# Banded attention and a softplus MLP on one core: quarter products in six token tiles, V rounded by its transfer, a maximum kept by the mask

## The chip, the cores and the metric

The kernel runs on one core of one Trainium2 chip. The core's engines each work through their own queue: TensorE (PE, matrix products, results in PSUM), VectorE (DVE), ScalarE (ACT), GpSimd (POOL) and SyncE (SP, which here only issues transfers). The metric is the device time of one execution in microseconds. Before the change it is 322.49 us, the median of 3 runs (322.43 to 322.93).

## The reference

The reference does attention with a band and a few global positions, reorders its result to tokens by features, and puts it through two matrix products with a softplus between them:

```python
def _attn_ref(q, k, v, global_idx):
    B, H, S, D = q.shape                       # 8, 8, 576, 64
    scores = (1.0 / np.sqrt(D)) * np.matmul(q, k.transpose(0, 1, 3, 2))
    mask = np.abs(pos[:, None] - pos[None, :]) <= 32
    mask = mask | is_global[:, None] | is_global[None, :]      # 8 global positions
    scores = np.where(mask, scores, -1000000000.0)
    scores = scores - np.max(scores, axis=-1, keepdims=True)
    attn = np.exp(scores)
    attn = attn / (np.sum(attn, axis=-1, keepdims=True) + 1e-09)
    return np.matmul(attn, v)

def _moe_ref(x, w_in, w_out):                  # x: 4608 x 512
    h = x @ w_in                               # 512 x 2048
    g = np.maximum(h, 0.0) + np.log1p(np.exp(-np.abs(h)))      # softplus
    return g @ w_out                           # 2048 x 512
```

## The kernel before

**Tiles.** The 4608 tokens are cut into 9 tiles of 512 (`m`, 0 to 8). The queries are cut into blocks of 32; a "pair" `n` (0 to 35, four per tile) is four such blocks with all 8 heads, and each block sees four key slots of 32 (previous, own, next, and the global keys). A batch `b` (0 to 7) is four and a half pairs.

**A pair's chain.** PE makes the scores (`s`, L1131) in two PSUM banks, one per half of the heads. For the first four pairs the mask is added by PE, DVE takes the maximum from PSUM, and ACT takes the exps with the maximum as a bias and keeps the sums (L1167). For the other 32 pairs DVE adds the mask on the way from PSUM to `st` (L1135, twice per pair) and takes the maximum (`m`, L1148), POOL subtracts it (L1154), ACT takes the exp of the whole pair (L1171), DVE sums it (`sm`, L1178) and inverts the sum (`rs`, L1180). Then POOL, for some pairs DVE, normalises into `pn` (L1186), DVE transposes it into `pt` (L1195), and PE multiplies with V (`xo`, L1297), which gives the token tile's input `xT` (L779). Rows of the global positions run beside it (`sg`, `pg`, `ov`, `vg`).

**A tile's products.** First product: for each of 16 column blocks of `w_in`, PE streams 512 tokens over 4 row blocks into `h` (L1334), and ACT writes the softplus to `g` (L1338), which exists once: the next tile's softplus overwrites it block by block. Second product, plain form (tiles 0 to 5): for each group of 128 tokens, 16 matmuls of 128x512 into one bank `o` (L1343), a copy to `osb` (L779) and a store. Second product in quarter products (tiles 6 to 8, `FAST = 6`, function `add_fast`): tokens, features and the inner dimension are halved, and the 2x2 by 2x2 block product is made from seven products of blocks instead of eight. Each of the seven is 8 x 2 matmuls of 128x256 (L1454). It needs four sums of quarters of `w_out`, made once, in two parts each (`add_sums`, "T"), and per tile four sums of quarters of `g`, in two parts each ("S", `combine`, L1403), made partly in place in `g` by DVE or POOL, each of them from the one before. Three of the results are added to an output on DVE (L1487). Sums of `w_out` lie in the staging buffers `stage` of q and k, and `s1` in that of V, so they wait until the last batch is loaded.

**Loads.** For batches 2 to 7, q, k and V come as fp32 into `stage` by SP's queue and are rounded to bf16 by POOL or ACT (`qk`, `vb`). V of batches 0 and 1 is rounded on its way by transfers that POOL issues (`load_rounded`, L500). `vb` exists twice. Stores of tiles 0 to 4 are issued by POOL, later ones by SP.

**What sets the order.** Each piece of work is recorded with `o.add` (its possible engines with costs, what it depends on, which buffers it opens and uses). `_Order.run` takes the pieces in the order that the table `ORDER` lists, each entry a piece and its engine, and emits them; each engine works in the order emitted. Up to 34 us of its own reckoning (`WARM`) it puts matmuls on an empty operand (`warm`, L786) into longer pauses of PE. The table is of the kernel itself; it is replaced whole.

Of the kernel before, what the change touches and what calls it, by code (L numbers as in the profile page):

```python
# [1658 lines left out]
```

## Time and profile before

| what | us |
|---|---|
| median of 3 runs | 322.49 (322.43 to 322.93) |
| the profiled execution's own time | 322.02 |
| its span, first to last instruction | 320.3 |
| PE busy | 309.9 (97%) |
| DVE busy | 249.0 (78%) |
| ACT busy | 229.7 (72%) |
| POOL busy | 217.7 (68%) |

The span is what the trace covers; the rest of an execution's time lies around it. In rows of a group (line, engine, operation, out<-in, shape, count) the numbers are busy us, mean ns of one, and the engine's idle time before them with what ended most of it. Rows of the chain of waits in order of time give start, us, and what ran, with its count. A matmul's own duration contains the pipeline's length: the streaming rate is read from a run of them in the chain.

### The profile page before, as it was taken

Reading aid. Unit: us, or ns where it says so; the run is one execution under the profiler, and the core shown is the slowest. Engines: PE = TensorE matmul, PEld = TensorE weight load, DVE = VectorE, ACT = ScalarE, POOL = GpSimd, SP = SyncE. Lnnn points to the kernel's source line nnn. Section 1 sums busy time; section 2 is a strip of 40 time slices with the busy share of each in tenths; the row PEclk is TensorE's granted clock in tenths of the full one; section 3 lists DMA queues with packets and bytes.
Section 4 is the critical chain, followed back from the end, with each engine's and each line's share of the span. In section 5 each row is a group of like instructions: output and inputs, shape, how many; then the busy total and the mean of one; then the engine's idle time right before and its main releaser. Section 6 shows DMA issues by size and latency. Waiting matters only on the chain.

```text
span 320.3 us, 12076 instructions
## 1 busy us (share of the span) xinstructions
PE 309.9 (97%) x5229; PEld 186.1 (58%) x5229; DVE 249.0 (78%) x438; ACT 229.7 (72%) x464; POOL 217.7 (68%) x186
## 2 busy tenths in 40 slices
PE   7889999999999999999999999999999999999995
PEld 6647965665565645544454455445544875685484
DVE  7987689976989898778988885897689666883063
ACT  7798847798698789579648946796199659726610
POOL 7994759892998687398788478499986385370220
PEclk9999999999999999999999999999999999999999
DMA  7999999999999899979996983710130010104003
GB/s 206 169 172 238 219 191 139 155 164 187 224 165 186 155 235 161 172 126 171 224 253 114 167 129 69 148 36 2 68 133 2 2 35 34 70 0 135 0 0 133
DMA packets 170335, 41.55 MB, mean 130 GB/s; under 512 B 153130, under 2 KB 168490, under 8 KB 170282
## 3 DMA queue, kind: packets, MB, share of 16 engines
q1 hardware_dynamic: 154920, 30.16, 49.5%
q0 software_dynamic: 15360, 10.62, 19.8%
q8 instruction: 41, 0.67, 0.9%
q14 instruction: 12, 0.10, 0.1%
q10 hardware_dynamic: 2, 0.00, 0.0%
HBM read 36.70 MB, written 9.44 MB: 144 GB/s over the span
## 4 chain that ended last, share of the span: by engine, by line
PE 89%; ACT 3%; POOL 3%; DMA 2%; DVE 1%; issue 0%; DVEq 0%; POOLq 0%
PE h L1334 38%; PE o L1343 27%; PE o L1454 11%; PE xo L1297 4%; PE s L1131 3%; DMA vb<-in_v_dram 2%; PE ov L1055 2%; POOL win L1525 2%; PE pick L945 1%; PE warm L786 1%; ACT st L1167 1%; ACT L1338 1%; PE sg L1029 1%; PE tr L913 1%; POOL pn L1186 1%; ACT g L1338 1%
## 5 line engine op out<-in xcount | busy, mean ns | idle before, releaser
L1334 PE MATMUL h<-xT,win 128*128 128x512 bf16 (+3 forms) x832 | 136.4, 313 | 1.4 <-ACT xT L779 0.7
L1338 ACT ACTIVATE g<-h 128x512 bf16<-128x512 f32 (+3 forms) x208 | 85.6, 490 | 35.1 <-PE h L1334 31.5
L1334 PEld LDWEIGHTS <-win 128*128 128x128 bf16 x832 | 70.7, 98 | 56.8 <-issue 3.1
L1343 PE MATMUL o<-wout,g 128*128 128x512 bf16 x384 | 93.3, 380 | 0.0
L1186 POOL TENSOR_TENSOR pn<-st,rs 128x1024 bf16<-128x1024 f32 (+1 forms) x40 | 68.7, 1736 | 31.2 <-DVE rs L1180 29.9
L1154 POOL TENSOR_TENSOR st<-st,m 128x1024 f32<-128x1024 f32 x32 | 60.4, 1895 | 24.9 <-DVE m L1148 23.9
L1343 PEld LDWEIGHTS <-g 128*128 128x128 bf16 x384 | 35.7, 98 | 39.5 <-issue 1.4
L1135 DVE TENSOR_TENSOR st<-s,mask 128x512 f32<-128x512 f32 x64 | 41.2, 678 | 12.2 <-PE s L1131 12.2
L1178 DVE TENSOR_REDUCE sm<-st 128x8 f32<-128x1024 f32 x32 | 38.3, 1196 | 2.2 <-ACT st L1171 2.0
L1148 DVE TENSOR_REDUCE m<-st 128x8 f32<-128x1024 f32 x32 | 38.3, 1206 | 0.3
L1171 ACT ACTIVATE st<-st 128x1024 f32<-128x1024 f32 x32 | 32.8, 1053 | 1.9 <-POOL st L1154 1.8
L1195 DVE STREAM_TRANSPOSE pt<-pn 128x512 int32<-128x512 int32 x36 | 24.6, 695 | 9.3 <-POOL pn L1186 9.2
L1454 PEld LDWEIGHTS <-g 128*128 128x128 bf16 x288 | 27.5, 98 | 5.7 <-ACT g L1338 0.3
L779 ACT COPY osb<-o 128x512 f32<-128x512 f32 x22 | 13.2, 600 | 13.6 <-PE o L1454 11.7
L779 ACT CAST xT<-xo 128x512 bf16<-128x512 f32 (+3 forms) x25 | 10.5, 475 | 15.2 <-PE xo L1297 15.1
L1338 ACT ACT_TABLE_LOAD x14 | 18.0, 1283 | 2.7 <-PE h L1334 2.4
L1454 PE MATMUL o<-wout,g 128*128 128x256 bf16 x144 | 19.5, 273 | 0.0
L1454 PE MATMUL o<-stage,g 128*128 128x256 bf16 x144 | 18.4, 273 | 0.0
L772 ACT ACTIVATE qk<-stage 128x1152 bf16<-128x1152 f32 (+1 forms) x14 | 16.9, 1217 | 1.6 <-DMA stage<-in_q_dram 1.6
L779 DVE CAST xT<-xo 128x512 bf16<-128x512 f32 (+3 forms) x27 | 12.6, 506 | 5.5 <-PE xo L1297 5.2
L1403 DVE TENSOR_TENSOR g<-g 128x1024 bf16<-128x1024 bf16 x8 | 7.8, 978 | 10.0 <-POOL stage L1403 9.9
L1171 ACT ACT_TABLE_LOAD x12 | 15.4, 1283 | 0.2
(145 smaller groups left out, 389.8 us busy)
## 6 DMA issues: line engine op xcount, KB each, us to landing
stage<-in_q_dram SPq DMA_DIRECT2D x48, 144.0 KB, 3.6
stage<-in_k_dram SPq DMA_DIRECT2D x48, 144.0 KB, 4.2
stage<-in_v_dram SPq DMA_DIRECT2D x48, 144.0 KB, 3.8
out_dram<-osb POOLq DMA_DIRECT2D x20, 256.0 KB, 3.8
out_dram<-osb SPq DMA_DIRECT2D x14, 256.0 KB, 2.5
...
```

The lines of the kernel that those rows point to most:

```text
L779: {"ACT": nc.scalar.copy, "DVE": V.tensor_copy, "POOL": nc.gpsimd.tensor_copy}[e](out, in_)
L1135: V.tensor_tensor(out=PS["st", n][:, h, :, :], in0=PS["s", n, h][:, :, :], in1=mask[:, h, j0:j0 + PB, :, :].rearrange("p j s i -> p j (s i ...
L1148: V.reduce_max(out=m[:], in_=flat(PS["st", n], h0, h1), axis=AX)
L1154: on(e).tensor_tensor(out=t, in0=t, in1=over(PS["m", n, y][:], SL * BL), op=OP.subtract)
L1171: nc.scalar.activation(out=t, in_=t, func=AF.Exp)
L1178: V.reduce_sum(out=sm[:], in_=flat(PS["st", n], h0, h1), axis=AX)
L1186: on(e).tensor_tensor(out=PS["pn", n][:, :, :, h0:h1].rearrange("p x s h -> p h x s"), in0=PS["st", n][:, h0:h1], in1=PS["rs", n, y][:].re ...
L1195: V.transpose(out=bass.AP(base.tensor, base.offset, ap=[list(base.ap[0]), [2 * STEP, PB // 2], [STEP + BL // 2, 2], [1, SL * BL]]), in_=PS ...
L1334: nc.tensor.matmul(out=h[:, :], lhsT=w_in_t[c // 4][:, kd, c % 4 * P:(c % 4 + 1) * P], rhs=PS["xT", m][:, kd, lo:hi], start=(kd == 0), sto ...
L1338: nc.scalar.activation(out=gs_[:, c, lo:hi], in_=PS[key][:, lo_of(c, hi - lo)], func=AF.Softplus)
L1343: nc.tensor.matmul(out=PS["o", m, ns, a][:, :], lhsT=gs_[:, kf, ns * P:(ns + 1) * P], rhs=w_out_t[kf // 4][:, kf % 4, a:z], start=(kf == 0 ...
L1454: nc.tensor.matmul(out=PS[key][:, 0 if i in split else n, :], lhsT=A[i](k, slice(n * P, (n + 1) * P)), rhs=Bs[i](k), start=first and y == ...
```

## The change

- Tiles 3, 4 and 5 make the second product in quarter products too (`FAST = 3`). Three of the four sums of `w_out` get buffers of their own (`fast`), the fourth overwrites a quarter of `w_out` once tiles 0 to 2 have read it, and `s1` lies in `early`, which the setup uses at the start. Nothing waits for the staging buffers any more. The stores of tiles 3 and 4 pass from POOL to SP.
- V of batches 2 to 7 is loaded by transfers of POOL's queue that round on the way; the fp32 staging buffer of V and its casts on POOL and ACT are gone.
- The mask of the 32 pairs is added by a DVE operation per block of 128 columns that also keeps the block's maximum, followed by an instruction that reads it out; the separate maximum is gone.
- In eight of these pairs (`BIASED`) the maximum is negated on DVE and ACT takes the exps block by block with it as a bias, and keeps the sums; the subtraction on POOL and the sum on DVE are gone there.
- Subtraction and normalisation may now be done by DVE or POOL in all tiles (six of each go to DVE).
- `pt` is packed more tightly (`STEP`), which changes no instruction's size. The table `ORDER` is a new one.

```diff
--- before
+++ after
-    STEP = 5 * BL
+    STEP = 4 * BL + BL // 2
+    BIASED = (8, 10, 12, 14, 16, 18, 20, 22)
     ORDER = (
...
-    stage = [const([P, HG * NC, 2, BL], FP32, f"stage{w}") for w in range(2)] + [const([P, 2, NJ, D], FP32, "stage2")]
+    stage = [const([P, HG * NC, 2, BL], FP32, f"stage{w}") for w in range(2)]
...
     def load_rounded(b, c):
         for h in range(2):
-            nc.gpsimd.dma_start(out=vb[b][quad(c), :, h * D:(h + 1) * D],
+            nc.gpsimd.dma_start(out=vb[b % 2][quad(c), :, h * D:(h + 1) * D],
                                 in_=SRC[2][b, HG * h + c].rearrange("(m i) d -> i m d", i=BL))
-
-    def load_v(eng, b, h, rs):
-        for c in rs:
-            eng.dma_start(out=stage[2][quad(c), h, :, :],
-                          in_=SRC[2][b, HG * h + c].rearrange("(m i) d -> i m d", i=BL))
...
-    idle = const([P, 512], BF16, "idle")
+    fast = {y: const([P, KF // 2, d_model // 2], BF16, f"fast{y}") for y in (0, 1, 3)}
+    idle = fast[0][:].rearrange("p k n -> p (k n)")[:, 0:512]
-    target = const([P, P], FP32, "target")
...
-    pos = const([P, S], FP32, "pos")
+    NF = 2 * NJ * NG + S + P + 2 * NG * NG + 3 * BL
+    early = const([P, max(NF, 1024)], FP32, "early")
...
         def ma(e, h):
-            V.tensor_tensor(out=PS["st", n][:, h, :, :], in0=PS["s", n, h][:, :, :],
-                            in1=mask[:, h, j0:j0 + PB, :, :].rearrange("p j s i -> p j (s i)"), op=OP.add)
+            if h == 0 or ("m", n, 0) not in PS:
+                PS["m", n, 0] = sb.tile([P, 2 * PB], FP32, tag=f"m{2 * PB}", name="m", bufs=ST)
+            for x in range(PB):
+                V.tensor_tensor_reduce(out=PS["st", n][:, h, x, :], in0=PS["s", n, h][:, x, :],
+                                       in1=mask[:, h, j0 + x, :, :].rearrange("p s i -> p (s i)"), scale=1.0, scalar=LOWEST,
+                                       op0=OP.add, op1=OP.max, accum_out=PS["m", n, 0][:, h * PB + x:h * PB + x + 1])
+            if biased:
+                m = PS["m", n, 0][:, h * PB:(h + 1) * PB]
+                V.reduce_max(out=m, in_=m.unsqueeze(2), axis=AX, negate=True)
...
-            if masked:
-                V.reduce_max(out=m[:], in_=PS["s", n, h0][:], axis=AX, negate=True)
-            else:
-                V.reduce_max(out=m[:], in_=flat(PS["st", n], h0, h1), axis=AX)
+            V.reduce_max(out=m[:], in_=PS["s", n, h0][:], axis=AX, negate=True)
...
+            elif biased:
+                t = flat(PS["st", n], h0, h1)
+                sm = PS["sm", n, y] = sb.tile([P, g], FP32, tag=f"sm{g}", name="sm", bufs=SB)
+                for x in range(g):
+                    nc.scalar.activation(out=t[:, x, :], in_=t[:, x, :], func=AF.Exp, bias=PS["m", n, y][:, x:x + 1], accum_out=sm[:, x:x + 1])
...
-                job = o.add({"POOL": (1905, 1905), "DVE": (1200, 1280)} if n < 4 * TP else {"POOL": (1905, 1905)}, lambda e, y=y: sub(e, y), [job], rank=at + 3, uses=[("st", n), ("m", n, y)], port=True)
+            elif biased:
+                job = T["ma", n, 1]
+            else:
+                job = o.add({"POOL": (1905, 1905), "DVE": (1200, 1280)}, lambda e, y=y: sub(e, y), [T["ma", n, 0], T["ma", n, 1]], rank=at + 3, uses=[("st", n), ("m", n, y)], port=True)
...
-    FAST = 6
+    FAST = 3
     KH, NH, DH = KF // 2, TT // 2, d_model // 2
-    fast = [flat(stage[w]).bitcast(BF16)[:, y * KH * DH:(y + 1) * KH * DH].rearrange("p (k n) -> p k n", k=KH) for w in range(2) for y in range(2)]
-    s1 = flat(stage[2]).bitcast(BF16)[:, 0:KH * NH].rearrange("p (k n) -> p k n", k=KH)
+    s1 = early[:, 0:KH * NH // 2].bitcast(BF16).rearrange("p (k n) -> p k n", k=KH)
 
     def wq(p, y, x):
         return w_out_t[2 * y + p][:, :, x * DH:(x + 1) * DH]
@@ -1403,21 +1404,22 @@
         on(e).tensor_tensor(out=out, in0=a, in1=b, op=op)
 
     def add_sums():
-        cost = {"DVE": (660, 720), "POOL": (2120, 2160)}
+        cost = {"DVE": (610, 670), "POOL": (2120, 2160)}
         SUB, ADD = OP.subtract, OP.add
-        t = lambda y, p: fast[y][:, 4 * p:4 * p + 4, :]
+        t = lambda y, p: wq(p, 0, 1) if y == 2 else fast[y][:, 4 * p:4 * p + 4, :]
+        free = [T["second", m, ns] for m in range(FAST) for ns in range(TP)]
...
-              4: lambda k: fast[3][:, k], 5: lambda k: fast[0][:, k], 6: lambda k: fast[1][:, k], 7: lambda k: fast[2][:, k]}
+              4: lambda k: fast[3][:, k], 5: lambda k: fast[0][:, k], 6: lambda k: fast[1][:, k], 7: lambda k: wq(k // 4, 0, 1)[:, k % 4]}
...
-                    add_load(b, 2, T["cast", b - 1, 2])
-                    add_cast(b, 2)
+                    add_rounded(b, [T["val", x] for x in old_vals(b - 2)] + had(("ov", b - 2)))
...
-    for key in list(T):
-        if key[0] == "T":
-            T[key]["deps"] += T["cast", B - 1, 0] + T["cast", B - 1, 1]
-        elif key[0] == "S" and key[2] == 1:
-            T[key]["deps"] += T["cast", B - 1, 2]
```

Three places where instructions move, by the order of each engine. On DVE, where the first pairs with the mask on DVE stand, before (`s` scores in PSUM, `st` in SBUF, `m` maxima):

```order
L1135 TENSOR_TENSOR st<-s,mask 128x512 x4
L1148 TENSOR_REDUCE m<-st 128x8
L1135 TENSOR_TENSOR st<-s,mask 128x512 x2
L1148 TENSOR_REDUCE m<-st 128x8 x2
L1135 TENSOR_TENSOR st<-s,mask 128x512
```

and after, the end of one of the eight pairs with a bias (line 1128 is the new `ma`, `m 128x1` the read-out):

```order
L1128 ISA st,m<-s,mask 128x128
L1128 ISA m 128x1
L1128 ISA st,m<-s,mask 128x128
L1128 ISA m 128x1
L1133 TENSOR_REDUCE m<-m 128x4
```

One pair was three instructions on DVE and is sixteen, or eighteen with a bias. On POOL, behind the normalisations of tile 1, before:

```order
L776 TENSOR_SCALAR qk<-stage_60 128x18x2x32
L1186 TENSOR_TENSOR pn<-st,rs 128x2x512
L779 CAST qk<-stage_61 128x18x2x32
L1352 DMA out_dram<-osb 128x512 x2
L1154 TENSOR_TENSOR st<-st,m 128x1024
```

and after (`vb` is V in bf16, `fast_81` a sum of `w_out`, `wout_130` a quarter of its rows):

```order
L781 TENSOR_SCALAR qk<-stage_60 128x18x2x32
L1354 DMA out_dram<-osb 128x512
L500 DMA vb_66<-in_v_dram 32x18x64 x2
L784 CAST qk<-stage_61 128x18x2x32
L1404 TENSOR_TENSOR fast_81<-wout_130 128x1024
L500 DMA vb_66<-in_v_dram 32x18x64 x4
```

V's transfers and a first sum of `w_out` stand between the casts of q and k and the stores. On PE, where the second product of tile 3 begins, before:

```order
L1334 LDWEIGHTS win_130
L1334 MATMUL h<-xT,win_130 128x512
L1343 LDWEIGHTS g
L1343 MATMUL o<-wout_134,g 128x512
```

and after (`early` holds `s1`):

```order
L1456 LDWEIGHTS g
L1456 MATMUL o<-wout_129,g 128x256
L1456 LDWEIGHTS early
L1456 MATMUL o<-fast_81,early 128x256
```

The 64 matmuls of 512 columns of a tile have become 112 of 256, and some take their stationary side from a sum. Over the whole program PE has 192 matmuls of 128x512 on the plain line instead of 384, 672 of 128x256 on the other instead of 336, and 19 long `warm` ones instead of 15. DVE has 44 sums of quarters instead of 21, POOL 12 instead of 11.

More of the change, by code (lines that the diff above doesn't have):

```diff
@@ L211, in due @@
                 d["on"] == "PE" or d["on"] == "DMA" and (not d["moves"] or not j["moves"] and d["cost"]["DMA"][0])
-                or d["on"] == "POOL" and d["moves"])
+                or d["on"] == "POOL" and d["moves"] and (j["moves"] or len(j["cost"]) == 1))
             t = max(t, j["hold"] + (d["at"] if same else d["end"] + self.HOP))
@@ L819, in add_rounded, with emit @@
             T["cast", b, 2].append(o.add({"POOL": (1360, 0)}, lambda e, c=c: load_rounded(b, c), T["cast", b, 2][-1:] or deps,
-                                         rank=-1, moves=1250, hold=0, sent=2))
-        T["load", b, 2] = T["cast", b, 2][-1]
+                                         rank=-1, moves=1250, hold=0, sent=2, late=900 if b else (1500, 1500, 1000, 400)[c]))
     def add_load(b, w, deps):
-        if w == 2:
-            for h in range(2):
-                T["half", b, h] = o.add({"DMA": (2200, 0)}, lambda e, h=h: load_v(nc.sync, b, h, range(R)), deps, rank=0, moves=4200 if b == EARLY else 2500, late=LATE + (SHARED - 1200 * h if b == EARLY else 0))
-            T["load", b, w] = T["half", b, 1]
-        else:
-            def emit(e):
-                if b == EARLY and "led" not in T:
-                    T["led"] = True
-                    follow(1, w_out_t[KF // 4 - 1])
-                load_qk(nc.sync, b, w, (0, 2, 1, 3))
-            T["load", b, w] = o.add({"DMA": (4400, 0)}, emit, deps + (had(("w_out", KF // 4 - 1)) if b == EARLY else []), rank=0,
-                                    moves=9000 if w else 8000, late=LATE + ((SHARED - 1500 * w) if b == EARLY else 0))
+        def emit(e):
+            if b == EARLY and "led" not in T:
+                T["led"] = True
+                follow(1, w_out_t[KF // 4 - 1])
+            load_qk(nc.sync, b, w, (0, 2, 1, 3))
+        T["load", b, w] = o.add({"DMA": (4400, 0)}, emit, deps + (had(("w_out", KF // 4 - 1)) if b == EARLY else []), rank=0,
+                                moves=9000 if w else 8000, late=LATE + ((SHARED - 1500 * w) if b == EARLY else 0))
     def add_parts(b):
@@ L851, in add_cast @@
     def add_cast(b, w):
-        if w == 2:
-            early = [T["val", x] for x in old_vals(b - 2)] + (had(("ov", b - 2)) if b >= 2 else [])
-        else:
-            early = had(("pick", b - 1, w)) if b == EARLY else T["turn", b - 1, w] + had(("pick", b - 1, w))
+        early = had(("pick", b - 1, w)) if b == EARLY else T["turn", b - 1, w] + had(("pick", b - 1, w))
         T["cast", b, w] = []
-        gate = [T["soft", b - 2, 9]] if w < 2 else []
+        gate = [T["soft", b - 2, 9]]
         for h in range(2):
             def emit(e, h=h):
-                if w == 2:
-                    copy(e, vb[b % 2][:, :, h * D:(h + 1) * D], stage[2][:, h, :, :])
-                else:
-                    c = slice(h * 2 * NC, (h + 1) * 2 * NC)
-                    (scaled, copy)[w](e, (qb, kb)[w][:, c, :, :].rearrange("p c d e -> p c e d"), stage[w][:, c, :, :])
-            n = NJ * D
-            cost = {"POOL": (1410, 1490), "ACT": (1380, 1480)}
-            if b == 0:
-                cost = {"POOL": (1150, 1250), "DVE": (760, 850)}
-            T["cast", b, w].append(o.add(cost, emit, [T["half", b, h] if w == 2 else T["load", b, w]] + early + gate, rank=10 * phase_of(b) + 4 if b else 1.5 if w == 2 else 0, port=True))
+                c = slice(h * 2 * NC, (h + 1) * 2 * NC)
+                (scaled, copy)[w](e, (qb, kb)[w][:, c, :, :].rearrange("p c d e -> p c e d"), stage[w][:, c, :, :])
+            T["cast", b, w].append(o.add({"POOL": (1410, 1490), "ACT": (1380, 1480)}, emit, [T["load", b, w]] + early + gate, rank=10 * phase_of(b) + 4, port=True))
     def add_prep(b):
@@ L1087, in add_global @@
             m0, m1 = 2 * SPANS[xs[0]][0], 2 * sum(SPANS[xs[-1]])
-            tps.append(o.add({"DVE": (985, 1070) if b else (680, 770)}, lambda e, m0=m0, m1=m1: tpg(e, m0, m1),
+            tps.append(o.add({"DVE": (1030, 1120) if b else (680, 770)}, lambda e, m0=m0, m1=m1: tpg(e, m0, m1),
                              [*exps, T["make_own"]] + ([T["ov", b - 1]] if b else []), rank=rank - 1, lead=lead))
@@ L1209, in add_pair @@
             for h in range(2):
-                T["ma", n, h] = o.add({"DVE": (607, 690)}, lambda e, h=h: ma(e, h), [T["sc", n], T["make_ends"]] + T["mask"], rank=at + 3,
-                                      uses=[("s", n, h), ("st", n)])
+                T["ma", n, h] = o.add({"DVE": (960, 1050) if biased else (840, 930)}, lambda e, h=h: ma(e, h), [T["sc", n], T["make_ends"]] + T["mask"], rank=at + 3,
+                                      uses=[("s", n, h), ("st", n)] + ([("m", n, 0)] if h else []), opens=[] if h else [("m8", ("m", n, 0))],
+                                      behind=[T["ma", n, 0]] if h else [])
         T["tp", n] = []
@@ L1223, in add_pair @@
                 T["sub", n, y] = job
-            T["ex", n, y] = o.add({"ACT": (990, 1070) if not masked else (1050, 1150) if n in SUMMED else (1390, 1490)}, lambda e, y=y: ex(e, y), [job, *gate],
-                                  rank=at + 2, uses=[("st", n)] + bank_ + ([("m", n, y)] if masked else []), table="exp",
+            T["ex", n, y] = o.add({"ACT": (3080, 3180) if biased else (990, 1070) if not masked else (1050, 1150) if n in SUMMED else (1390, 1490)}, lambda e, y=y: ex(e, y), [job, *gate] + ([T["ma", n, 0]] if biased else []),
+                                  rank=at + 2, uses=[("st", n)] + bank_ + ([("m", n, y)] if masked or biased else []), table="exp",
@@ L1226, in add_pair @@
                                   opens=[] if summed else [(f"sm{g}", ("sm", n, y))])
-            job = o.add({"DVE": (1360, 1480) if not masked else (740, 840) if n in SUMMED else (100, 200)}, lambda e, y=y: su(e, y), [T["ex", n, y]], rank=at + 1,
+            job = o.add({"DVE": (100, 200) if biased else (1360, 1480) if not masked else (740, 840) if n in SUMMED else (100, 200)}, lambda e, y=y: su(e, y), [T["ex", n, y]], rank=at + 1,
                         uses=[("st", n)] + ([] if summed else [("sm", n, y)]), opens=([(f"sm{g}", ("sm", n, y))] if summed else []) + [(f"rs{g}", ("rs", n, y))])
@@ L1229, in add_pair @@
             T["su", n, y] = job
-            job = o.add({"POOL": (1040, 1080), "DVE": (700, 780)} if n < TP else {"POOL": (1905, 1905), "DVE": (1250, 1330)} if n < 4 * TP else {"POOL": (1905, 1905)}, lambda e, y=y: no(e, y), [job], rank=at,
+            job = o.add({"POOL": (1040, 1080), "DVE": (700, 780)} if n < TP else {"POOL": (1905, 1905), "DVE": (1250, 1330)}, lambda e, y=y: no(e, y), [job], rank=at,
                         opens=[("pn", ("pn", n))] if y == 0 else [], uses=[("st", n), ("rs", n, y)] + ([("pn", n)] if y else []),
@@ L1419, in add_fast @@
         SUB = OP.subtract
-        cost = {"DVE": (660, 720), "POOL": (2120, 2160)}
+        cost = {"DVE": (610, 670), "POOL": (2120, 2160)}
         N = slice(0, NH), slice(NH, 2 * NH)
```

35 lines of the change are left out of this document (21 added, 14 removed), and 144 rows, old and new, of the table ORDER.

## The prediction

> **What bounds the kernel now.** I read the page first (busy time, then the chain), then the stretch of each token tile, then the rows of single groups. The page's head and its chain of waits:
>
> ```profile
> span 320.3 us, 12076 instructions
> PE 309.9 (97%) x5229; PEld 186.1 (58%) x5229; DVE 249.0 (78%) x438; ACT 229.7 (72%) x464; POOL 217.7 (68%) x186
> PE 89%; ACT 3%; POOL 3%; DMA 2%; DVE 1%; issue 0%; DVEq 0%; POOLq 0%
> ```
>
> PE is busy for 97% of the span and carries 89% of the chain; nothing else has more than 3%. A share of busy time can hide waits, so I looked at stretches: the opening, and the stretch in which the first tile with quarter products begins.
>
> ```profile
> 0.00:36.00 36.00, 30.26 (x722) 23.86 (x723) 28.80 (x96) 29.66 (x112) 26.84 (x53) 1.00 1.19 196
> 36.00:72.00 36.00, 36.00 (x728) 23.56 (x727) 30.83 (x52) 27.23 (x72) 29.54 (x29) 1.00 1.20 171
> 216.00:252.00 36.00, 35.16 (x585) 18.85 (x584) 27.87 (x45) 25.95 (x40) 28.21 (x17) 1.00 0.13 46
> ```
>
> The columns are the stretch and its length, then busy us of PE, weight loads, DVE, ACT and POOL, then clock, DMA share and GB/s. Behind the opening PE has no gap (36.00 of 36.00), at a granted clock of 1.00; 0.84 us are lost where tile 6 begins. So time goes down only if PE gets less to stream, and it goes up by whatever makes PE wait. The next five rows cut the trace at the first PE instruction of `xo` (probabilities times V) of tiles 3 to 8, so that each row is one token tile's worth of steady work:
>
> ```profile
> 128.33:160.03 31.70, 31.70 (x520) 15.72 (x528) 26.29 (x42) 24.21 (x36) 23.57 (x17) 1.00 0.97 173
> 160.03:193.08 33.05, 33.05 (x557) 16.30 (x564) 27.71 (x44) 21.97 (x33) 22.78 (x16) 1.00 0.87 161
> 193.08:225.85 32.77, 32.77 (x526) 16.21 (x533) 25.44 (x41) 23.40 (x36) 27.08 (x19) 1.00 0.29 62
> 225.85:256.60 30.75, 29.91 (x502) 18.01 (x509) 23.42 (x39) 22.63 (x35) 21.28 (x13) 1.00 0.15 53
> 256.60:287.12 30.52, 30.45 (x424) 20.59 (x432) 23.35 (x34) 21.26 (x30) 19.24 (x11) 1.00 0.11 37
> ```
>
> The first three hold tiles 3 to 5 with the plain second product, mean 32.51; the last two hold tiles 6 and 7 with seven quarter products, mean 30.64, with nearly as much attention in them. Before's own trace thus holds both forms of the second product, 1.87 us a tile apart.
>
> **The change part by part.** *Quarter products in tiles 3 to 5.* These rows of the chain give the streaming rates:
>
> ```profile
> 53.85 2.59 PE o L1343 x12
> 304.73 11.80 PE o L1454 x108
> 22.84 0.68 DVE xT L779 x3
> 24.88 1.52 ACT st L1167 x8
> ```
>
> A plain 128x512 matmul takes 2.59/12 = 0.216 us, a quarter one (128x256) 11.80/108 = 0.1093 us. A plain tile has 64 (4 row groups of 16), a quarter one 7 x 8 x 2 = 112. Per tile 64 x 0.216 = 13.82 goes and 112 x 0.1093 = 12.24 comes: 1.58 us less, and **4.8 us** less for three tiles (192 out, 336 in). The tile rows would give 3 x 1.87 = 5.6. I take 4.8 and keep 5.6 for the low end.
>
> *What quarter products cost elsewhere.* Per tile 8 sums of softplus quarters (128x1024 bf16) and 3 additions of a product to an output, and once 8 sums of w_out quarters, now far earlier.
>
> ```profile
> L1403 DVE TENSOR_TENSOR g<-g,stage 128x1024 bf16<-128x1024 bf16 x6 | 4.1, 689 | 0.7 <-DVE g L1403 0.5
> L1487 DVE TENSOR_TENSOR osb<-o,osb 128x512 f32<-128x512 f32 x7 | 4.7, 675 | 2.1 <-PE o L1454 1.1 <-ACT osb L779 0.9
> L1135 DVE TENSOR_TENSOR st<-s,mask 128x512 f32<-128x512 f32 x64 | 41.2, 678 | 12.2 <-PE s L1131 12.2
> L1148 DVE TENSOR_REDUCE m<-st 128x8 f32<-128x1024 f32 x32 | 38.3, 1206 | 0.3
> L1178 DVE TENSOR_REDUCE sm<-st 128x8 f32<-128x1024 f32 x32 | 38.3, 1196 | 2.2 <-ACT st L1171 2.0
> L779 DVE CAST xT<-xo 128x128 bf16<-128x128 f32 x9 | 2.1, 284 | 0.7 <-PE xo L1297 0.5
> L1036 DVE TENSOR_REDUCE gnb<-gm 128x1 f32<-128x2 f32 x8 | 1.2, 154 | 0.3
> L779 DVE COPY osb<-o 128x512 f32<-128x512 f32 x14 | 9.3, 673 | 3.4 <-PE o L1454 2.5 <-PE o L1343 0.9
> L1167 ACT ACTIVATION_READ_ACCUMULATOR st<-s,m 128x1 f32 x32 | 7.7, 240 | 0.0
> L1171 ACT ACTIVATE st<-st 128x1024 f32<-128x1024 f32 x32 | 32.8, 1053 | 1.9 <-POOL st L1154 1.8
> L1171 ACT ACT_TABLE_LOAD x12 | 15.4, 1283 | 0.2
> ```
>
> The order gives DVE 23 more of the sums (21 to 44) and 9 more additions: 23 x 0.689 + 9 x 0.675 = 21.9 us, less 4 copies of `osb` (2.7). It also takes 6 more subtractions and 6 normalisations (one half-size) that POOL did. No such 1024-wide fp32 operation of two tensors is in this trace on DVE; between 1.2 (the reduction of 1024) and 1.36 (two adds of 512), about 14.5 us. All of it lies beside PE as long as DVE has room.
>
> *Mask with maximum.* Out go 64 adds and 32 maxima, 41.2 + 38.3 = 79.5 us. In come 256 pairs: one 128x128 add that also keeps the maximum, and a one-element read-out. Neither is in the trace. Lowest: the main one as the 128x128 cast from PSUM when such casts follow each other, (0.68 - 0.284)/2 = 0.198 us, with the read-out free: 256 x 0.198 = 51 us. Highest: both alone, without overlap, 0.284 + 0.154 = 0.438: 112 us. ACT's read-out is not free either: 8 rows of L1167 (4 exps, 4 read-outs) take 1.52, so 0.38 a pair. I take 0.275 (0.198 and half of a lone small operation, since neighbours on DVE overlap): 70.4 us, 9 less than now. [...]
>
> DVE's total: 249.0 - 79.5 + 70.4 + 21.9 - 2.7 + 14.5, less 8 sums of probabilities (9.6), plus 16 small sign changes (2.5) = 266 us, 84% of the span. Per tile: 25.2 now (126.20/5), -9.9 for the old mask over 8 tiles, +8.8 for the new, +3.3 for the rest = 27.4, below PE's 30.6.
>
> *Eight pairs' exps on ACT.* Eight times 8 exps of 0.38 = 24.3, instead of 8 x 1.05 = 8.4; four fewer table loads of 1.283 (5.1); two V casts less and four copies of `osb` more nearly cancel: ACT goes from 229.7 to about 240. Tiles with two such pairs get 2 x 2 = 4 us on 22.7. That is under 30.6 too. POOL loses 14 subtractions in all.
>
> *V rounded by transfer.*
>
> ```profile
> L1186 POOL TENSOR_TENSOR pn<-st,rs 128x1024 bf16<-128x1024 f32 x32 | 60.5, 1901 | 29.6 <-DVE rs L1180 28.3 <-ACT g L1338 0.8 <-DVE pt L1195 0.5
> L1154 POOL TENSOR_TENSOR st<-st,m 128x1024 f32<-128x1024 f32 x32 | 60.4, 1895 | 24.9 <-DVE m L1148 23.9 <-DMA stage<-in_v_dram 0.7
> L779 POOL CAST vb<-stage 128x1152 bf16<-128x1152 f32 x10 | 11.5, 1153 | 4.8 <-PE xo L1297 4.8
> L500 POOL DMA_DIRECT2D vb<-in_v_dram x16 | 11.0, 697 | 1.8 <-DMA wout<-in_moe_w_out_dram 1.7
> stage<-in_v_dram SPq DMA_DIRECT2D x48, 144.0 KB, 3.8
> vb<-in_v_dram POOLq DMA_DIRECT2D x16, 72.0 KB, 5.4
> L1352 POOL DMA_DIRECT2D out_dram<-osb x20 | 11.4, 570 | 0.6 <-ACT osb L779 0.6
> stage<-in_q_dram SPq DMA_DIRECT2D x48, 144.0 KB, 3.6
> ```
>
> POOL gives up 10 casts (11.5) and 14 subtractions (26.5), 6 normalisations (10.6), 8 stores of 0.57 (4.6), and issues 48 transfers more, 48 x 0.697 = 33.5: 198 us with the rest as it is, less than 217.7. The transfers leave SP's queue, whose q and k loads come forward, and are queued on POOL between normalisations. They may start only when the buffer of two batches ago is read, so a wait like the 4.8 us above (2 times) stays in POOL's queue, with the normalisations behind it; `pt` on DVE, and then `xo` on PE, wait for those. Landing takes 5.4 us instead of 3.8 and a cast of 1.15. Hidden, the price is 0. If the cover goes, PE loses up to the longest such wait, 2.5 us (half of 4.8), per batch. I take 0, since POOL has 9 us free per tile (22.8 busy of 31.8 in the five rows above). The stores of tiles 3 and 4 pass to SP's queue, between the last q and k loads; even if a load's eight pieces ran one after another, 8 x 3.6 = 29 us, a store would be late by less than the tile's 30.6 after which its buffer, one of four, is wanted again: 0.
>
> *Opening.* PE runs the same rows up to the first `xo`; then four more warming matmuls of 512, 0.86 us, stand where this execution's chain runs over ACT's exps (24.88) and not over PE. Between 0 and 0.86 I take **+0.3**.
>
> *First quarter-product tile.* Its start cost PE 0.84 us at tile 6:
>
> ```profile
> 240.61 1.89 PE L1334 MATMUL h<-xT,win 128*128 128x512 bf16 x8 [0.64 <-ACT g L1338]
> ```
>
> It moves to tile 3. There the other engines carry the same work and DMA is fuller (0.97 against 0.15). From -0.84 (it vanishes) to +1.7 (tiles 3 to 5 each pay about as much), I take **+0.5**.
>
> Sum: -4.8 + 0.3 + 0.5 = **-4.0 us**. The profiled execution took 322.02 with a span of 320.3 (1.7 outside it); the span becomes 316.3, that execution 318.0, and the median, which lies 0.47 above it at 322.49, about **318.5**. Own range: 322.49 - 5.6 = 316.9 to 322.49 - 4.8 + 0.86 + 1.7 = 320.3.
>
> **The rivals.** *DVE becomes the bound (slower).* With a pair at x us, DVE has 18.6 + 32x us per tile (27.4 - 8.8, and 32 pairs); this passes PE's 30.6 at x = 0.375. At the upper bound, 0.438, it is 32.6: 2.0 us over per tile, about 6 tiles, 12 us, less the 4.0: some 330. For it: the instruction count and ACT's 0.38. Against it: DVE's neighbours overlap, as the casts show. Chance 0.07.
>
> *V comes late (slower).* In-order POOL waits for PE's last read of the old V and normalisations stand behind it. From 4.0/6 = 0.67 us exposed per batch the gain is gone; if three of six batches cost 2.5, the time is 318.5 + 7.5 = 326. For it: the POOL wait of 4.8, the 5.4 us landing. Against it: POOL's idle time and V being wanted only after scores, exps and a normalisation. Chance 0.11.
>
> *Dependent sums hold PE.* The second and later products need sums of sums, on DVE or POOL, and the softplus buffer is single. If every quarter-product tile adds 0.5 us, 318.5 + 3 = 321.5. For it: the 0.84 us at tile 6. Against it: tile 7's row, 30.45 busy of 30.52. Chance 0.13.
>
> *No change:* something else already sets the period of tiles 3 to 5, and 322.5 stays. Against it: PE without a gap there. Chance 0.06.
>
> **How the numbers follow.** The forecast has 0.63. A measurement of this kernel can tell 0.2%, 0.65 us, from no change. Faster by more: the forecast, 0.63, and nearly all of the third rival, 0.12, so 0.75; within: 0.07; slower: 0.07 + 0.11 = 0.18. The range starts a little under the own range, at 316.6, and ends at 322.6, which takes in the third rival and no change, and leaves out the two slower ones.
>
> **What would show it.** Right: PE still near 97%; 672 matmuls of 128x256 on the line of quarter products at 0.109 us; `xo` to `xo` near 30.7 in tiles 3 to 5; DVE's pair under 0.3 us. Wrong: idle time of PE ended by DVE (`s` banks not freed, sums of `g`) or by `vb`; POOL waiting for `xo` longer than 2.5; a period of tile 3 above 32; DVE busy over 30 in a tile.

## The result, and the profile after

The changed kernel is slower, by 1.6%: 328.2 us median (327.2 to 334.4, 4 runs) against 322.7 (322.4 to 323.2, 4 runs). The ratio is 1.0158 (95% interval 1.0126 to 1.0190); the run of 334.4, one of e5 (327.2) and the profiled execution of e8 were disturbed and are left out of the ratios. Forecast were 318.5 us and a gain. The profiled execution took 327.74 with a span of 325.3.

The head of the page and its chain of waits, for the kernel after:

```profile
span 325.3 us, 12888 instructions
PE 306.7 (94%) x5344; PEld 201.7 (62%) x5377; DVE 257.0 (79%) x904; ACT 244.4 (75%) x579; POOL 201.4 (62%) x198
PE 66%; DVE 12%; ACT 8%; DMA 5%; POOL 5%; issue 2%; SPq 0%; ACTq 0%; DVEq 0%; POOLq 0%
```

PE has less to stream than before (306.7 against 309.9), and no other engine is full, but PE's share of the chain fell from 89% to 66% and DVE's rose from 1% to 12%. The span, cut at the first `xo` of batch 1's values, of tile 3, of tile 6 and of tile 8, shows where. The stretch and its length come first, then busy us of PE, weight loads, DVE, ACT and POOL, then the granted clock. Two stretches of before (its later ones are in the prediction), then five of after:

```profile
0.00:60.36 60.36, 54.62 (x1170) 39.18 (x1170) 50.15 (x132) 45.92 (x155) 46.86 (x75) 1.00 1.25 189
60.36:128.26 67.90, 67.90 (x1239) 40.12 (x1239) 59.52 (x93) 57.81 (x119) 51.67 (x36) 1.00 0.98 182
```

```profile
0.00:62.02 62.02, 55.28 (x1165) 40.26 (x1176) 47.41 (x200) 48.63 (x159) 45.53 (x76) 1.00 1.29 187
62.02:135.96 73.94, 68.97 (x1231) 40.91 (x1240) 63.31 (x231) 58.93 (x175) 58.48 (x48) 0.98 0.99 143
135.96:230.19 94.23, 90.99 (x1681) 58.44 (x1687) 81.00 (x298) 79.08 (x158) 65.77 (x54) 1.00 0.80 115
230.19:292.55 62.36, 62.05 (x940) 42.14 (x945) 54.16 (x162) 43.67 (x66) 28.34 (x21) 1.00 0.26 45
292.55:325.35 32.80, 29.39 (x335) 19.93 (x336) 11.07 (x18) 14.09 (x24) 3.24 (x2) 0.98 0.19 65
```

| stage | before | after | difference | forecast |
|---|---|---|---|---|
| opening | 60.36 | 62.02 | +1.7 | +0.3 |
| up to tile 3's `xo` | 67.90 | 73.94 | **+6.0** | 0 |
| tiles 3 to 5 | 97.52 | 94.23 | -3.3 | -4.3 |
| tiles 6 and 7 | 61.27 | 62.36 | +1.1 | 0 |
| the rest | 33.2 | 32.8 | -0.4 | 0 |

A gain where the quarter products are is there, though a mark cuts through tile 5's products (see the account of the prediction below). The loss is in a stage that has none of them, in which PE had been busy without a gap. Of PE's waits over the whole span (us, times, longest), these are the three longest single ones behind the start-up. The first and the third lie in that stage, at 81.3 and 110.9; the second lies in the opening, at 37.3:

```profile
PE pick L941 <- DVE picked L784: 2.0, 1, 2.0
PE tr L902 <- DVE qk L779: 1.3, 1, 1.3
PE s L1121 <- DVE kx L784: 1.1, 1, 1.1
```

The longest, before the `pick` at 81.28, in the chain (start, us, what):

```profile
72.62 4.44 DVE pn L1185
...
78.37 1.28 DVE qx L874
79.65 1.26 DVE kx L878
80.91 0.32 DVE picked L784
...
81.28 0.27 PE pick L941
```

One normalisation on DVE (`pn` of pair 8, one of those that the change moved there) took 4.5 us where another took 1.3, and all that DVE has behind it, up to the gathered keys that PE wants, came later for it. It waited for no semaphore in that time. The timelines of DVE and POOL at that place (start, us, what) show what ran beside it:

```profile
72.54 4.51 DVE L1185 TENSOR_TENSOR pn<-st,rs 128x1024 bf16<-128x1024 f32 x1
```

```profile
72.33 1.48 POOL L784 CAST qk<-stage 128x1152 bf16<-128x1152 f32 x1
73.73 2.13 POOL L1404 TENSOR_TENSOR fast<-wout 128x1024 bf16<-128x1024 bf16 x1
75.80 2.65 POOL L500 DMA_DIRECT2D vb<-in_v_dram  x4
```

It ended at 77.05, 1.2 us after POOL's sum of `w_out` quarters had (75.86), which is about what it took beside transfer issues alone (1.31 at 148.47). So it stood still while POOL computed, through a cast and the sum right behind it. At 107.60 a copy that took 0.24 us at 82.52 took 3.27 (below). At 206.80 another normalisation was held, though less long than POOL's unbroken run. DVE, then POOL's first two of three subtractions in a row:

```profile
206.80 2.37 DVE L1185 TENSOR_TENSOR pn<-st,rs 128x1024 bf16<-128x1024 f32 x1
```

```profile
206.12 1.90 POOL L1148 TENSOR_TENSOR st<-st,m 128x1024 f32<-128x1024 f32 x1 [0.66 <-DVE m L1128]
207.98 2.92 POOL L1148 TENSOR_TENSOR st<-st,m 128x1024 f32<-128x1024 f32 x1
```

It ended 1.2 us after the first subtraction, and the second one took 2.92 us instead of 1.90. So here DVE was let in after one operation of POOL, and POOL stood instead. In e5, where the normalisation at 72.5 is on POOL, the longest on DVE takes 2.38 us. PE did not wait for it. Why DVE was let in here and not between the cast and the sum is not shown.

The clock went with the wait of 2.0 us. Two neighbouring stretches of 3.41 us, the number behind POOL's being the granted clock:

```profile
78.56:81.97 3.41, 1.37 (x9) 0.77 (x8) 3.05 (x4) 0.62 (x2) 1.56 (x3) 1.00 1.76 204
81.97:85.38 3.41, 3.41 (x119) 1.97 (x117) 1.55 (x9) 1.25 (x3) 0.00 (x0) 0.50 1.15 281
```

After a stretch with PE busy for 1.37 of 3.41 us came one at a granted clock of 0.50. Behind the `pick`, 8 products of 384 columns took 2.02 us, 0.25 each, where the next 24 took 4.11, 0.17 each. My estimate is that the stretch loses another 1.7 us, half of its 3.41. Before had a lower clock at its very end alone (0.51 in its last 3.17 us). The stage's waits of 2.0 and 1.1 us, one of 0.4 at 78.4, and these 1.7 make 5.2 of the 6.0.

### The profile page after: what moved, and what is told of

Its sections match the earlier page's. It is cut to its first block, busy times and chain, and to the rows that moved or that the text cites. A ratio compares the mean times of both kernels' runs of the same rounds, so it can differ in the third digit from the quotient of the medians.

```text
span 325.3 us, 12888 instructions
## 1 busy us (share of the span) xinstructions
PE 306.7 (94%) x5344; PEld 201.7 (62%) x5377; DVE 257.0 (79%) x904; ACT 244.4 (75%) x579; POOL 201.4 (62%) x198
## 4 chain that ended last, share of the span: by engine, by line
PE 66%; DVE 12%; ACT 8%; DMA 5%; POOL 5%; issue 2%; SPq 0%; ACTq 0%; DVEq 0%; POOLq 0%
PE h L1336 30%; PE o L1456 18%; PE o L1345 8%; PE xo L1299 3%; POOL pn L1185 3%; PE s L1121 2%; DVE st L1128 2%; DMA stage<-in_q_dram 2%; DMA vb<-in_v_dram 2%; ACT st L1170 2%; DVE pn L1185 2%; DMA out_dram<-osb 2%; POOL win L1527 1%; ACT g L1340 1%; ACT L1340 1%
## 5 line engine op out<-in xcount | busy, mean ns | idle before, releaser
L1340 ACT ACTIVATE g<-h 128x512 bf16<-128x512 f32 (+3 forms) x208 | 87.1, 486 | 33.7 <-PE h L1336 33.2
L1185 POOL TENSOR_TENSOR pn<-st,rs 128x1024 bf16<-128x1024 f32 (+1 forms) x34 | 58.5, 1728 | 47.2 <-DVE rs L1179 42.4
L1128 DVE CUSTOM_DVE_ANT_0 st<-s,mask 128x128 f32<-128x128 f32 x256 | 56.8, 283 | 13.3 <-PE s L1121 13.2
L1456 PE MATMUL o<-wout,g 128*128 128x256 bf16 x384 | 48.9, 273 | 0.0
L1148 POOL TENSOR_TENSOR st<-st,m 128x1024 f32<-128x1024 f32 x18 | 35.1, 1954 | 22.3 <-DVE m L1128 22.1
L1345 PE MATMUL o<-wout,g 128*128 128x512 bf16 x177 | 43.6, 379 | 1.9 <-issue 1.1
L500 POOL DMA_DIRECT2D vb<-in_v_dram x64 | 43.2, 683 | 2.4 <-DMA wout<-in_moe_w_out_dram 2.2
L1167 ACT ACTIVATE st<-st,m 128x128 f32<-128x128 f32 x64 | 24.7, 393 | 0.0
L1456 PE MATMUL o<-fast,g 128*128 128x256 bf16 x192 | 24.4, 273 | 0.3 <-ACT osb L784 0.3
L1128 DVE DVE_READ_ACCUMULATOR2_ANT m<- 128x1 f32 x256 | 21.1, 82 | 0.0
L1489 DVE TENSOR_TENSOR osb<-o,osb 128x512 f32<-128x512 f32 (+1 forms) x20 | 12.5, 627 | 7.1 <-PE o L1456 4.9
L784 DVE CAST xT<-xo 128x128 bf16<-128x128 f32 (+3 forms) x29 | 12.7, 465 | 6.8 <-PE xo L1299 6.6
```

Of the source, the lines that this page charges most:

```text
L500: nc.gpsimd.dma_start(out=vb[b % 2][quad(c), :, h * D:(h + 1) * D], in_=SRC[2][b, HG * h + c].rearrange("(m i) d -> i m d", i=BL))
L784: {"ACT": nc.scalar.copy, "DVE": V.tensor_copy, "POOL": nc.gpsimd.tensor_copy}[e](out, in_)
L1128: V.tensor_tensor_reduce(out=PS["st", n][:, h, x, :], in0=PS["s", n, h][:, x, :], in1=mask[:, h, j0 + x, :, :].rearrange("p s i -> p (s i) ...
L1148: on(e).tensor_tensor(out=t, in0=t, in1=over(PS["m", n, y][:], SL * BL), op=OP.subtract)
L1185: on(e).tensor_tensor(out=PS["pn", n][:, :, :, h0:h1].rearrange("p x s h -> p h x s"), in0=PS["st", n][:, h0:h1], in1=PS["rs", n, y][:].re ...
L1340: nc.scalar.activation(out=gs_[:, c, lo:hi], in_=PS[key][:, lo_of(c, hi - lo)], func=AF.Softplus)
```

## The experiments

Times are ratios to the kernel before, measured beside each (323.1 to 323.7 us there), with 95% intervals where there were several runs. The kernel after was not measured again beside them, so a comparison with its 1.0158 is rougher than one with before. **Theory H:** a DVE operation stands while POOL computes, and single such holds make the loss. **Rival O:** the opening is late, all queues are out of step, and one hold only stands for another. **Rival V:** V by transfer is late.

### What holds DVE, and what it costs

*e1_sum_later* moves the sum on POOL:

```diff
 L784 CAST qk<-stage_61 128x18x2x32
-L1404 TENSOR_TENSOR fast_81<-wout_130 128x1024
 L500 DMA vb_66<-in_v_dram 32x18x64 x4
 L1354 DMA out_dram<-osb 128x512 x3
+L1404 TENSOR_TENSOR fast_81<-wout_130 128x1024
```

> Edit: one w_out sum on POOL (the one that ran at 73.7 to 75.9 us) goes behind the three output stores that follow it; nothing else moves. Theory H (DVE's normalisation of pair 8 is held while POOL computes on whole SBUF tiles): only POOL's cast, which ends at 73.8, holds it any more, so it takes about 2.5 us instead of 4.51, PE's idle stretch before the pick at 78.9 falls from 2.2 to about 0.2 us, the half-clock stretch of 3.41 us at 82 goes, and the time falls by 2.0 + 1.7 = 3.7 us, to about 324.5. If POOL's transfer issues hold DVE as well, the normalisation stays at 4 us or more and nothing is won. Rival O (the opening's 1.4 us puts all queues out of step, and one hold only stands for another): a wait of the same size appears elsewhere, 327.5 to 328.5. Rival V (V by transfer is late): no change, 328.

*e5_norm_pool* moves the normalisation (`L1185` leaves DVE's list and stands on POOL):

```diff
 L500 DMA vb_66<-in_v_dram 32x18x64 x2
+L1185 TENSOR_TENSOR pn<-st,rs 128x2x512
 L784 CAST qk<-stage_61 128x18x2x32
```

> Edit: the normalisation of pair 8 goes back from DVE to POOL, ahead of POOL's cast; nothing else moves. Theory H: no hold there at all; PE's 2.2 us before the pick and the half-clock stretch (1.7 us lost) go: about 324 us. POOL's cast and w_out sum come 1.9 us later, which costs nothing by this theory. Rivals O and V: 327.5 to 328.5.

*e6_two_sums* doubles the suspected cost:

```diff
 L784 CAST qk<-stage_61 128x18x2x32
 L1404 TENSOR_TENSOR fast_81<-wout_130 128x1024
+L1404 TENSOR_TENSOR fast_81<-wout_129 128x1024
 L500 DMA vb_66<-in_v_dram 32x18x64 x4
```

> Edit: a second w_out sum (2.13 us on POOL, from about 110 us) is put right behind the one that ran at 73.7, so that POOL computes 2.1 us longer while pair 8's normalisation stands on DVE. Theory H: the normalisation takes 4.51 + 2.1 = 6.6 us, PE idles 2.1 us more there, 330.3 us, or up to 331.5 if the half-clock stretch grows too. Rivals O and V, by which such a hold is not what costs the time: 328 to 328.5.

*e2_kx_act* leaves that place alone and takes the other held operation from DVE to ACT:

```diff
 L953 STREAM_TRANSPOSE qkg_73<-placed 128x256
-L784 COPY kx_71<-qkg_73 128x40x8
 L784 CAST xT<-xo 128x384 x2
```

> Edit: the copy of the gathered keys into kx for batch 3 (DVE, 107.60, 3.27 us in the kernel after) goes to ACT, at the same place of the order. Theory H: that copy was held by POOL; on ACT it takes some 0.4 us, PE's 1.34 us before the scores at 110.9 go, 326.9 us. Rival O: PE waits at the same place for something else, 328.

The same stage, from the first `xo` to tile 3's, in the traces of e1, e5, e6 and e2, in this order:

```profile
61.80:132.67 70.87, 67.78 (x1230) 40.34 (x1239) 61.95 (x231) 58.95 (x175) 58.49 (x48) 1.00 1.06 154
```

```profile
63.55:133.46 69.91, 67.50 (x1230) 40.37 (x1238) 58.94 (x230) 58.76 (x173) 60.16 (x49) 1.00 1.03 150
```

```profile
61.27:138.18 76.91, 69.86 (x1230) 41.27 (x1238) 65.38 (x231) 58.99 (x175) 58.49 (x48) 0.96 1.00 145
```

```profile
61.24:133.91 72.67, 68.88 (x1231) 40.89 (x1239) 60.26 (x230) 59.25 (x176) 58.54 (x48) 0.98 1.03 150
```

| kernel | stage, us | against after's 73.94 | ratio to before |
|---|---|---|---|
| e1 | 70.87 | -3.1 | 1.010 (1.0052 to 1.0149) |
| e5 | 69.91 | -4.0 | 0.9995 (0.9962 to 1.0028) |
| e6 | 76.91 | +3.0 | 1.0244 (1.0184 to 1.0303) |
| e2 | 72.67 | -1.3 | 1.0058 (1.0021 to 1.0095) |

Theory H gave 6.6 us for the normalisation in e6. DVE's and POOL's timelines of e6:

```profile
71.81 6.59 DVE L1185 TENSOR_TENSOR pn<-st,rs 128x1024 bf16<-128x1024 f32 x1
```

```profile
71.61 1.47 POOL L784 CAST qk<-stage 128x1152 bf16<-128x1152 f32 x1
73.02 4.21 POOL L1404 TENSOR_TENSOR fast<-wout 128x1024 bf16<-128x1024 bf16 x2
77.18 2.01 POOL L500 DMA_DIRECT2D vb<-in_v_dram  x3
```

POOL computes 2.1 us longer, DVE is held 2.1 us longer, and 6.82 us at half clock follow (81.05 to 87.87, granted 0.50). In e1 the normalisation took 2.38 us, as expected with the cast alone before it. That is 1.1 more than its 1.3, and about what e1's stage is longer than e5's (1.0). In e5 the hold and the half clock are gone (1.00 over the stage). The rivals had 328 for all of these: both fall as the cause of this loss. e2 and e5 came out lower than theory H had them (1.0058 where 326.9 us would be 1.013, 0.9995 where 324 would be 1.004), and lower than their stage alone explains; the length of a stage is that of one execution. V is not late at all: no wait of PE in the kernel after names `vb`.

### Is the copy held by transfer issues too?

In the kernel after, timelines of DVE and POOL:

```profile
107.60 3.27 DVE L784 COPY kx<-qkg 128x320 bf16<-128x320 bf16 x1
```

```profile
105.44 2.13 POOL L1404 TENSOR_TENSOR fast<-wout,fast 128x1024 bf16<-128x1024 bf16 x1
107.51 1.33 POOL L500 DMA_DIRECT2D vb<-in_v_dram  x2
108.86 1.91 POOL L1185 TENSOR_TENSOR pn<-st,rs 128x1024 bf16<-128x1024 f32 x1
```

The copy, which waits for DVE alone, came just behind the sum's end and still stood until POOL's normalisation was over, through two issues of V. *e7_copy_first* lets it come earlier, *e13_pause* takes away the normalisation behind the issues:

```diff
+L953 STREAM_TRANSPOSE qkg_73<-placed 128x256
+L784 COPY kx_71<-qkg_73 128x40x8
 L1194 STREAM_TRANSPOSE pt<-pn 128x2x2x128
-L953 STREAM_TRANSPOSE qkg_73<-placed 128x256
-L784 COPY kx_71<-qkg_73 128x40x8
```

> Edit: in the kernel after, on DVE the transpose of the gathered keys and their copy into kx for batch 3 go ahead of one transpose of pn (0.67 us), so that the copy stands ready while POOL's w_out sum still runs, and not just behind its end as before. Theory H1 (a waiting DVE operation is let in at the first end of a POOL computation that is followed by transfer issues, since issues do not hold it): the copy takes 0.5 to 1.0 us instead of 3.27 and ends with the sum, at about 107.8. Theory H2 (issues hold it as well, once POOL has gone on without a pause): it ends with POOL's normalisation behind the issues, at about 110.9, 3.9 us. The time is not the point: pt, now behind it, is late by up to 1.2 us either way, so 327 to 329 by H1 and 329 or more by H2.

```diff
 L784 COPY kx_71<-qkg_73 128x40x8
+L1185 TENSOR_TENSOR pn<-st,rs 128x2x512
 L784 CAST xT<-xo 128x384 x2
```

> Edit: in the kernel after, POOL's normalisation behind the two transfer issues at 107.5 to 108.8 goes to DVE, right behind the copy into kx; POOL then has nothing to compute behind the issues for some us. If the copy is held until POOL, after a run without a pause, stands still: it ends with the second issue, at about 108.9, 1.3 us instead of 3.27. If it is held only by computation and let in at the first end of an issue: 0.6 us. If it is held until POOL's next computation has ended, whenever that is: 3 us or more. The normalisation on DVE (1.3 us) then holds back the casts of xo, so the time is no measure here.

One execution each: 330.14 us and 324.45 us. The copy and POOL in e7:

```profile
105.89 3.86 DVE L784 COPY kx<-qkg 128x320 bf16<-128x320 bf16 x1
```

and in e13:

```profile
106.29 0.24 DVE L784 COPY kx<-qkg 128x320 bf16<-128x320 bf16 x1
```

```profile
106.22 1.34 POOL L500 DMA_DIRECT2D vb<-in_v_dram  x2
110.82 1.90 POOL L1148 TENSOR_TENSOR st<-st,m 128x1024 f32<-128x1024 f32 x1 [3.26 <-DVE m L1128]
```

By e7 alone I would have said that issues hold a copy (H2, 3.9 us expected, 3.86 measured). e13 corrects it: beside the same issues, with nothing ready to compute behind them, the copy took 0.24 us, less than any of my three readings allowed. So at this place issues alone hold nothing, and a computation that stands ready behind two issues holds the copy during the issues already. e13 is one execution, and how POOL comes by that is not settled by these runs.

### Do the pieces add up, and is anything else in the way?

*e8_two_moves* is e5 and e2 together. *e9_evict_later* adds a third move, from this chain of the kernel after, in which an eviction on DVE waits for a store to land, with a pair's masks behind it:

```profile
136.73 5.03 DMA out_dram<-osb
141.88 0.69 DVE osb L784
```

```diff
 L784 CAST xT<-xo 128x512 x2
-L784 COPY osb<-o 128x512
 L1128 ISA st,m<-s,mask 128x128
...
 L1128 ISA m 128x1
+L784 COPY osb<-o 128x512
```

> Edit: both single moves at once, pair 8's normalisation to POOL and the copy of batch 3's gathered keys to ACT. Theory H: the holds are separate losses and add up; the first move alone gave 0.9995 of before, the copy costs PE 1.34 us more, so 0.9955 of before, some 321.3 where before has 322.7. Rival O (whatever is freed is waited for elsewhere): 0.999 to 1.000.

> Edit: the kernel with both moves, and on DVE one eviction of o into osb (which waited 2.9 us for the store of an earlier tile's osb to land, with the masks of pair 19 behind it) goes behind those masks. If that wait is what makes PE lose 0.65 us at 141 and some 0.4 more beside it: 0.7 to 1.1 us less than the kernel with both moves, 0.993 of before. If PE there waits for something else: no difference, 0.9955.

e8 gave 0.9984 (0.9967 to 1.0000). That is not told apart from e5's 0.9995, and it takes in the rival's 0.999 to 1.000 and leaves out the 0.9955 of theory H; no trace of e8 shows its stages. e9 gave **0.9951 (0.9926 to 0.9977)**, 0.5% under before, and under the kernel after by far. Its stages:

```profile
0.00:61.86 61.86, 55.70 (x1174) 39.34 (x1174) 48.46 (x200) 48.73 (x159) 45.41 (x76) 1.00 1.26 184
61.86:130.49 68.63, 68.22 (x1239) 40.36 (x1239) 55.95 (x229) 59.42 (x176) 60.49 (x49) 1.00 1.09 159
130.49:223.94 93.45, 91.40 (x1686) 58.59 (x1686) 81.14 (x298) 79.26 (x158) 65.83 (x54) 1.00 0.79 115
```

The bad stage went from 73.94 to 68.63, 5.3 less, which is the sum of the two single moves in their traces (4.0 + 1.3): in the traces the two losses add up, and e8's time alone does not show it. Tiles 3 to 5 took 0.8 us less than in after, and 0.5 less than in e2 (93.97), which has after's eviction. Against before, 3.0 us are now won over tiles 3 to 7 (155.8 for 158.8), and 1.5 are still lost in the opening and 0.7 in the second stage.

*e10_short_exps*, on top of e8, asks whether ACT's load makes the waits of PE that remain at 215 to 221 in e9. The biased pairs' probabilities are not computed in it:

```diff
-                for x in range(g):
-                    nc.scalar.activation(out=t[:, x, :], in_=t[:, x, :], func=AF.Exp, bias=PS["m", n, y][:, x:x + 1], accum_out=sm[:, x:x + 1])
+                nc.scalar.activation(out=t, in_=t, func=AF.Exp, scale=0.0)
+                nc.scalar.activation(out=sm[:], in_=PS["m", n, y][:], func=AF.Exp, scale=0.0)
```

> Edit: the kernel with both moves, and the eight biased pairs' exps (8 small exps and 8 read-outs each, about 3.0 us on ACT) are left out but for one exp of 1024 and one of 8 elements, without bias and sums, so the probabilities of these pairs are not computed: some 14 us less on ACT. Theory A (ACT, loaded by these pairs, is what PE waits for between 214 and 225, 2.2 us): 2 us less than the kernel with both moves, 0.989 of before. As the prediction had it (ACT's work lies beside PE): no difference over 0.3 us, and the PE waits at 214 to 225 stay, because they come from the order of ACT's work there and not from its amount.

The ratio is 0.9967 (0.9941 to 0.9992), within e8's interval and far from the 0.989 of theory A. From tile 5's `xo` to tile 6's, where that stretch lies, ACT is busy for 25.05 us (25.06 in e9), so what it was spared lies ahead of there. The three waits of PE in the stretch are the same as in e9, to the digit:

```profile
PE pick L934 <- ACT qk L784: 0.7, 1, 0.7
PE ov L1044 <- ACT g L1340: 0.5, 1, 0.5
PE ov L1044 <- DVE pgt L1035: 0.4, 1, 0.4
```

So the biased pairs' exps are not what PE waits for there. Whether it is the order of ACT's work there, or the rest of it, was not tested.

*e11_opening* (8 matmuls of two first products, of 256 columns and not 384 as its expectation has it, ahead of the transpose that waits for batch 1's q, on top of e9) and *e12_twelve_back* (the moved normalisations and subtractions back on POOL, in the kernel after):

```diff
+L1336 LDWEIGHTS win_128
+L1336 MATMUL h<-xT,win_128 128x256
...
 L902 LDWEIGHTS qk
 L902 MATMUL tr<-ident,qk 128x128
...
-L1336 LDWEIGHTS win_128
-L1336 MATMUL h<-xT,win_128 128x256
...
```

> Edit: on top of the kernel with both moves and the later eviction, two first products of 384 columns (8 matmuls, 1.3 us of PE) go ahead of the transpose that waits at 36 us for batch 1's q load; nothing else moves. If that wait (1.44 us in the kernel after, 0.6 to 1.0 in the others) is a loss of its own: 0.6 to 1.0 us less than the kernel before this edit (0.9951 of before), 0.992 to 0.993. If batch 1's transposes and casts on DVE are then late by the same amount (the chain goes on over q and not over PE): 0.995 to 0.997.

> Edit: in the kernel after, the five large normalisations and six subtractions that the change had moved from POOL to DVE go back to POOL, each at its place of the order (the half-size one stays); all other parts of the change stay. Theory H: the holds at 72.5, 206.8 and 270.1 go, and with the first PE's 2.8 us and the half-clock 1.7 us; the copy at 107.6 stays held. Against that stand 11 x 1.9 = 21 us more on POOL, in order, so that normalisations come later: between 0 and 4 us. So 323.7 to 327.7, at or under the kernel after. If DVE's load, and not its holds, was what cost the time: clearly under before, 320. If POOL has no room for it: above the kernel after, 329 or more.

e11 gave 0.9953 (0.9937 to 0.9968), the same as e9. The wait of 0.8 us at 36 went, another of 0.5 came behind it, and the first stage was 62.04 long for 61.86 (its first `xo` of all came 0.5 later), which speaks for the second reading: the chain there goes over batch 1's q and not over PE. e12 gave 1.0117 (1.0072 to 1.0161), a little under the kernel after and far above before. The hold at 72.5 is gone, but PE waited 1.4 us for a copy into `kx` (1.1 in after), and 1.1 us more before a `pick`. Giving all of it back to POOL is no cure; moving the one operation that meets POOL's work is.

## Why the prediction was wrong

**The step that failed** is the cost of the moved normalisations and subtractions: "about 14.5 us. All of it lies beside PE as long as DVE has room." The durations were right where nothing was in the way, and the group rows of after show where not:

```profile
L1148 DVE TENSOR_TENSOR st<-st,m 128x1024 f32<-128x1024 f32 x6 | 7.2, 1198 | 0.0
L1185 DVE TENSOR_TENSOR pn<-st,rs 128x1024 bf16<-128x1024 f32 x5 | 11.2, 2246 | 0.0
```

1.2 us for the subtractions, inside the 1.2 to 1.36 given; 2.25 on average for the normalisations, through one each of 4.51, 2.37 and 1.74 beside two of 1.3. What followed from the 4.51 is the wait of 2.0 us, one of 0.4 and the half clock; without that hold (e5) the stage is 4.0 us shorter. Room on DVE was there (79% busy). What I did not ask is what POOL does at that moment, and how long its run is: the normalisation left POOL, and the `w_out` sums, "now far earlier", came to stand on POOL just where it now ran. I counted the 23 more sums on DVE and overlooked that the ones at 73.7 and 105.4 run on POOL. The rivals were others; none was a hold between two engines that are both far from full. Before's own page showed such holds: the prediction priced a sum of quarters by the row of 689 ns, and another row of the same size beside it has 978, through one sum of 2.32 and one of 1.39 us, each beside a sum on POOL:

```profile
L1403 DVE TENSOR_TENSOR g<-g 128x1024 bf16<-128x1024 bf16 x8 | 7.8, 978 | 10.0 <-POOL stage L1403 9.9
```

```profile
310.01 2.32 DVE L1403 TENSOR_TENSOR g<-g 128x1024 bf16<-128x1024 bf16 x1
309.67 2.12 POOL L1403 TENSOR_TENSOR g<-g 128x1024 bf16<-128x1024 bf16 x1 [8.53 <-PE o L1454]
```

What such a hold costs is in the traces: 4.51 us for about 1.3 us of work at 72.5, through a cast and the sum behind it, and 6.59 in e6, through a cast and two sums, while the one at 206.8 ended with one subtraction. What in the two engines makes one stand for the other is not shown. The prediction priced the moved operations by their own time alone, though the change moves work between just these two engines. Of the 9.0 us between the forecast span (316.3) and the measured one (325.3), this stage makes 6.0, the quarter products 2.1 and the opening 1.4; the end of the program gives 0.4 back.

**V by transfer, price 0:** right for V itself. The 48 more issues were not free in one place, where two of them stand between POOL's sum and its normalisation and the copy was held through them; moving the copy (e2) shortened the stage by 1.3 us.

**Mask with maximum, 0.275 us a pair:** too dear. The pairs in after's chain follow each other at 0.21:

```profile
142.57 0.20 DVE st L1128
142.76 0.01 DVE m L1128
142.77 0.20 DVE st L1128
```

That is near the lowest bound, 0.198. So DVE came to 257.0 instead of 266 with the holds in it, and "DVE becomes the bound" had nothing for it. ACT (244.4 for 240) and POOL (201.4 for 198) were near.

**Quarter products, -4.8 and +0.5:** the right sign, and too large. In e9's chain a run of them:

```profile
181.52 6.66 PE o L1456 x60
```

0.111 each, not 0.1093, so 13.82 - 112 x 0.111 = 1.4 a tile and 4.2 in all. The stage table cannot be set against this as it stands. In e9, 288 of the 336 quarter matmuls of tiles 3 to 5 lie ahead of the mark of tile 6, so 48 of tile 5's run behind it (5.3 us); in before, 13 of its 64 plain ones do (2.8). So 2.5 us of tile 5 are counted with tiles 6 and 7, which is more than their +1.1. Over tiles 3 to 7 together e9 is 3.0 us under before and after 2.2, where -4.3 was forecast. PE stands for 2.1 us there in e9 and for 0.9 in before; these 1.2 more, in place of the +0.5, and the 4.2 give the 3.0. The forecast gain was thus too large by 1.3 us in e9 and by 2.1 in after. The 5.6 of the tile rows was no firm bound either: the rows of tiles 6 and 7 hold 80 score matmuls a tile, those of tiles 3 to 5 139.

**Opening, +0.3:** measured +1.7 (e9 +1.5), above the 0.86 that I gave as its end. PE waits for batch 1's q there, 1.3 us in after, 0.8 in e9 and 0.5 in e11; before shows no such wait. That wait does not explain it all: with the same opening e2 took 61.24 us, and e5 63.55 without any such wait, so one execution tells the size to 1 or 2 us only. **Store of a tile's output, 0:** wrong by some 0.5 us, by e9 against e2. I had asked whether its buffer is wanted a tile later; it was wanted by an eviction on DVE 2.9 us too early, with masks behind that.
